# Two channel products by Strassen's scheme, in two sweeps over the batches

## The chip, the cores and the metric

The kernel runs on one core of one Trainium2 chip. A time is device microseconds of that core, from the start of the program to its end. Five engines run beside each other, each through its own instructions in the order written: TensorE (PE; its weight loads are listed as PEld), VectorE (DVE), ScalarE (ACT), GpSimd (POOL), and SyncE (SP), whose queue issues all the DMAs here. They meet at semaphores only.

## The reference

Three blocks follow one another: chunked attention (8 batches, 8 heads, 576 tokens, 64 channels a head, chunks of 64), a gated block, and a mixer. The change touches the last, of which this is all:

```python
xt = x.transpose(0, 2, 1)
h = np.maximum(xt @ w_tok1, 0.0) @ w_tok2          # 576 -> 256 -> 576 tokens
u = x + h.transpose(0, 2, 1)
h2 = np.maximum(u @ w_ch1, 0.0) @ w_ch2            # 512 -> 1536 -> 512 channels
return (u + h2).astype(np.float32)
```

`x` is (8, 576, 512). The two products of the last-but-one line are called the channel products here, the two of `h` the token products.

## The kernel before, in words

Every float32 operand of a product is split into two float32r parts, hi (a copy by ACT) and lo (the remainder, by a subtraction on DVE or POOL), and a product is made of three: hi x hi, hi x lo, lo x hi (`PASSES`), summed in PSUM.

Phase A makes attention and the gated block of all batches; its order of issue is written out in strings of words (`FIRST`, `STEADY`, `LAST`), each word an operation and its block. It also rounds the mixer's weights to float32 and leaves them in DRAM, and each batch's result, channels by tokens, in DRAM (`x2d`). `LAST` overlaps the last gated block with the start of phase B: words `f` and `g` load and split weights, `bl`, `bn` load and transpose token rows of batch 0, `k`, `m` are its token products, `D` copies an output of the gated block out of PSUM.

Phase B is the mixer. It goes through batches, two halves of 288 tokens (`HALF`), and 12 blocks `f` of 128 of the 1536 channels. `b_ch1` (L798, matmuls L804) is 12 matmuls (4 blocks of 128 channels x 3 passes) of 288 columns; ACT and DVE take the relu and split it (L810, L811). `b_ch2` (L815, L823), two blocks later, is 12 matmuls into four PSUM banks that stay open over all 12 blocks; then DVE adds u and transposes (L829, L836), and SP stores. The token products of the next batch stand in between (`b_load` L710, `b_nat` L721, `b_tok1` L738, `b_tok2` L773, which adds x and splits u, L790 to L792). Both weights stay in SBUF, hi and lo; their pieces are split during batch 0 (`b_split`, L82). The main loop sets the order:

```python
    for i, (b, h, f) in enumerate(seq):
        b_ch1(b, h, f)
...
        if i >= 2:
            b2, h2, f2 = seq[i - 2]
            b_ch2(b2, h2, f2)
```

The order of issue is program order on every engine. A tile of a pool waits, when its slot comes round again, until the slot's last users are done; within a tile, waits go by the part that is read or written.

## Time and profile before

| | |
|---|---|
| three runs | 1305.63, 1309.06, 1310.22 us |
| median | 1309.06 us |
| profiled execution: its span (no other time is given for it) | 1307.3 us |
| instructions | 25669 |
| matmuls | 10571 |
| of them channel products (L804, L823) | 2304 + 2304 |
| granted TensorE clock, mean | 0.987 |

The profile is of one execution. Its page gives each engine's busy time, the span in 40 slices, the chain of work that ended last, and groups of instructions: line, engine, operation, tiles (out<-in), shapes, count, then busy time, mean duration in ns, idle time ahead of the group and what ended it. Matmuls are pipelined: the duration of one is a latency, and what a matmul costs in a stream is the step from one to the next. Rows of the timeline begin with start and length in us. Rows by stretch give the stretch and its length, busy time and instructions of PE, PEld, DVE, ACT and POOL, granted clock, DMA share and GB/s.

### The profile page before, as it was taken

Reading aid. Unit: us, or ns where it says so; the run is one execution under the profiler, and the core shown is the slowest. Engines: PE = TensorE matmul, PEld = TensorE weight load, DVE = VectorE, ACT = ScalarE, POOL = GpSimd, SP = SyncE. Lnnn points to the kernel's source line nnn. Section 1 sums busy time; section 2 is a strip of 40 time slices with the busy share of each in tenths; the row PEclk is TensorE's granted clock in tenths of the full one; section 3 lists DMA queues with packets and bytes.
Section 4 is the critical chain, followed back from the end, with each engine's and each line's share of the span. In section 5 each row is a group of like instructions: output and inputs, shape, how many; then the busy total and the mean of one; then the engine's idle time right before and its main releaser. Section 6 shows DMA issues by size and latency. Waiting matters only on the chain.

```text
span 1307.3 us, 25669 instructions
## 1 busy us (share of the span) xinstructions
PE 1259.0 (96%) x10571; PEld 1195.4 (91%) x10571; DVE 662.8 (51%) x1357; ACT 419.1 (32%) x822; POOL 160.8 (12%) x151
## 2 busy tenths in 40 slices
PE   6789999999989999999999999999999999999998
PEld 4588998888888989999999999999999999999998
DVE  6986868596777655357332442433333324423421
ACT  2653536363544343345121221211211212212111
POOL 2743223333233000000000000000000000000000
PEclk7889999999999999999999999999999999999999
DMA  8947274867677330255303203222132042032100
GB/s 170 177 97 155 53 170 98 194 133 180 150 142 172 65 77 20 65 144 172 75 4 69 45 13 57 45 35 45 35 69 45 2 69 45 10 60 45 20 16 22
DMA packets 391993, 106.53 MB, mean 81 GB/s; under 512 B 361794, under 2 KB 376706, under 8 KB 391876
## 3 DMA queue, kind: packets, MB, share of 16 engines
q1 hardware_dynamic: 391876, 104.89, 37.9%
q8 instruction: 83, 1.36, 0.5%
q14 instruction: 34, 0.28, 0.1%
HBM read 78.48 MB, written 26.35 MB: 80 GB/s over the span
## 4 chain that ended last, share of the span: by engine, by line
PE 74%; DVE 12%; DMA 5%; SPq 3%; issue 2%; ACT 2%; POOL 1%; DVEq 0%; POOLq 0%; ACTq 0%
PE ps_a L823 23%; PE ps_c L804 23%; PE ps_s L589 6%; PE ps_o L615 5%; PE ps_v L477 4%; PE ps_u L785 4%; PE ps_h L746 3%; SPq L292 3%; PE ps_u L566 2%; DVE qkT L320 2%; DMA c_f<-ctmp 1%; DVE v L543 1%; DMA qk_raw<-in_k_dram 1%; DVE ctmp L152 1%; DVE sm L364 1%
## 5 line engine op out<-in xcount | busy, mean ns | idle before, releaser
L804 PE MATMUL ps_c<-u,c 128*128 128x288 f32 x2304 | 337.4, 295 | 0.4 <-ACT u L791 0.4
L823 PE MATMUL ps_a<-h,c 128*128 128x288 f32 x2304 | 337.8, 295 | 0.0
L823 PEld LDWEIGHTS ps_a<-h,c 128*128 128x128 f32 x2304 | 316.9, 188 | 4.1 <-issue 1.7
L804 PEld LDWEIGHTS ps_c<-u,c 128*128 128x128 f32 x2304 | 316.9, 189 | 1.2 <-ACT u L791 0.8
L811 DVE SCALAR_TENSOR_TENSOR h<-ps_c,h 128x288 fp32r<-128x288 f32 x192 | 87.3, 455 | 389.5 <-ACT h L810 389.5
L810 ACT ACTIVATE h<-ps_c 128x288 fp32r<-128x288 f32 x192 | 79.0, 411 | 446.3 <-PE ps_c L804 446.3
L589 PE MATMUL ps_s<-ws,vn 128*128 128x288 f32 x768 | 112.1, 302 | 8.6 <-ACT ut L576 6.0
L615 PE MATMUL ps_o<-g,w_out 128*128 128x288 f32 x768 | 110.4, 302 | 9.0 <-ACT x2o L622 8.3
L589 PEld LDWEIGHTS ps_s<-ws,vn 128*128 128x128 f32 x768 | 106.2, 193 | 11.0 <-ACT ut L576 7.7
L615 PEld LDWEIGHTS ps_o<-g,w_out 128*128 128x128 f32 x768 | 105.5, 193 | 10.9 <-ACT x2o L622 9.1
L566 PE MATMUL ps_u<-xt,w_in 128*128 128x288 f32 x768 | 105.8, 296 | 0.0
L566 PEld LDWEIGHTS ps_u<-xt,w_in 128*128 128x128 f32 x768 | 103.3, 189 | 0.9 <-POOL w_in L188 0.2
L477 PE MATMUL ps_v<-w_in,xt 128*128 128x512 f32 x384 | 94.6, 403 | 3.3 <-ACT xt L421 1.9
L477 PEld LDWEIGHTS ps_v<-w_in,xt 128*128 128x128 f32 x384 | 72.4, 191 | 21.5 <-ACT xt L421 2.2
masks.py:197 POOL MEMSET ident<- 128x128 f32 x2 | 0.4, 207 | 681.9 <-DVE xn L729 681.6
L370 POOL TENSOR_TENSOR e<-e,sm 128x512 f32<-128x512 f32 (+1 forms) x40 | 39.1, 977 | 229.3 <-DVE sm L366 193.9
L785 PE MATMUL ps_u<-w,h 128*128 128x288 f32 x384 | 61.0, 295 | 0.3 <-DVE xh L790 0.3
L785 PEld LDWEIGHTS ps_u<-w,h 128*128 128x128 f32 x384 | 54.1, 188 | 0.5 <-DVE xh L790 0.5
L162 POOL TENSOR_TENSOR craw<-craw 128x512 f32<-128x512 f32 (+3 forms) x41 | 41.6, 1014 | 101.7 <-DVE craw L154 51.2
L163 POOL TENSOR_TENSOR ctmp<-ctmp,craw 128x512 f32<-128x512 f32 (+3 forms) x41 | 50.8, 1240 | 3.2
L791 ACT CAST u<-xh 128x288 fp32r<-128x288 f32 x64 | 27.7, 433 | 68.3 <-DVE xh L790 68.3
L746 PE MATMUL ps_h<-xn,w 128*128 128x512 f32 x192 | 49.1, 392 | 0.0
(110 smaller groups left out, 1294.8 us busy)
## 6 DMA issues: line engine op xcount, KB each, us to landing
craw<-in_moe_w_ch_dram SPq DMA_DIRECT2D x24, 512.0 KB, 4.3
x_raw<-x2d SPq DMA_DIRECT2D x160, 64.0 KB, 2.7
qk_raw<-in_q_dram SPq DMA_DIRECT2D x128, 72.0 KB, 3.4
qk_raw<-in_k_dram SPq DMA_DIRECT2D x128, 72.0 KB, 2.9
...
out_dram<-oT SPq DMA_DIRECT2D x240, 36.0 KB, 1.7
...
```

Source lines behind the costliest of these rows:

```text
L162: nc.gpsimd.tensor_tensor(out=f32(high), in0=f32(low), in1=f32(high), op=ALU.mult)
L163: nc.gpsimd.tensor_tensor(out=t, in0=t, in1=f32(high), op=ALU.add)
L477: nc.tensor.matmul(ps, lhsT=self.xt[kc][:, p, 128 * ti:128 * ti + 128], rhs=w_in_t[r][:, kc, DM:2 * DM], start=kc == 0 and n == 0, stop=kc ...
L566: nc.tensor.matmul(ps[:, h, 0:HALF], lhsT=w_in_t[r][:, kc, 128 * m:128 * m + 128], rhs=self.xt[kc][:, p, HALF * h:HALF * h + HALF], start= ...
L589: nc.tensor.matmul(ps[:, h, 0:HALF], lhsT=lhsT, rhs=rhs[:, HALF * h:HALF * h + HALF], start=n == 0, stop=n == len(ops) - 1)
L615: nc.tensor.matmul(ps[:, h, 0:HALF], lhsT=w_out_t[r][:, kc, 128 * m:128 * m + 128], rhs=self.g[p][:, kc, h], start=kc == 0 and n == 0, sto ...
L746: nc.tensor.matmul(ps[kk], lhsT=PB["w1"][r][:, m, ksl], rhs=xn[:, p], start=m == 0 and n == 0, stop=False)
L785: nc.tensor.matmul(ps, lhsT=h1[:, kk, p, 128 * m:128 * m + 128], rhs=PB["w2"][r][:, kk, HALF * h:HALF * h + HALF], start=n == 0, stop=n == 5)
L804: nc.tensor.matmul(ps, lhsT=PB["c1", f // 4][r][:, kc, 128 * (f % 4):128 * (f % 4) + 128], rhs=u[p][:, kc], start=n == 0, stop=n == 11)
L810: nc.scalar.activation(out=h2[:, 0], in_=ps, func=ACTF.Relu)
L811: nc.vector.scalar_tensor_tensor(out=h2[:, 1], in0=ps, scalar=0.0, in1=f32(h2[:, 0]), op0=ALU.max, op1=ALU.subtract)
L823: nc.tensor.matmul(acc[m], lhsT=PB["c2"][r][:, f, 128 * m:128 * m + 128], rhs=h2[:, p], start=f == 0 and n == 0, stop=f == NF - 1 and n == 2)
```

## The change

Each channel product is cut into blocks of half size in its three dimensions: 256 of 512 channels, two column halves of the weight, two halves of the tokens. Instead of eight block products, seven are made, of sums and differences of blocks (`SETS` says which weight block goes with which), and further sums behind them give the four result blocks. A product's matmuls still have 128x128 weights and 288 columns.

Both products no longer go hand in hand. A first sweep goes over all batches and makes h = u @ w_ch1 in three column groups of 2 x 256 (the relu comes with the copy or later, by block), 21 block products of 12 matmuls a batch (`ch1`, `ch1_out`), and stores h to DRAM (`hd`), as u is (`u2d`). A second sweep goes over all batches again and makes the other product, 7 block products of 36 matmuls a batch (`ch2`, `ch2_out`), from h and u loaded back (`h_load`, `u_load`).

- Sums of weight blocks (`Comb`): the six pieces of w_ch1 (pairs for the three groups) and of w_ch2 are loaded, added, split, and added on, on POOL, with the copies on ACT; the first pair during `LAST` (words `y`, in place of the `f` and `g` of channel weights), the second ahead of the sweep, the third in group 1 of batch 0. Those of w_ch2 take the same tiles when the last batch's groups are done with them; the last pair is summed on DVE, and split by DVE and POOL, between the sweeps.
- Sums of u blocks (`comb_u`): on DVE, in the last group of the batch before; remainders on DVE, two of seven on POOL.
- Sums of h blocks (`comb_h`): three products ahead, each on 1728 columns; remainders on DVE, two of seven on POOL. `less(o, x, y)` is max(x, 0) - y.
- Token products (`tok_steps`): 19 steps a batch, one after each block product of the first sweep.
- Results of the last product go out by DVE transposes for all batches; the path by TensorE for the last one (`b_out_last`) is dropped.
- Buffers: 3 PSUM tiles of two banks for the products; 4 slots `c` shared by weight pieces and results on their way out; 3 slots `hb`.

The diff, cut to its core:

```diff
 V0 R0 R1 V1 V2 R3 R2 r1 r0 F U0 G r2 R4 r3 U1 E0 r4 rs rq N0 N3 i0 N1 U2 Q0 i1 E1 U3 open N2
 i2 N4 i4 f0 Q1 f1 i3 bl0 Q3 E2 Q2 Q4 W0 xl0 f2 E3 M0 f3 f4 H0 g0 W1 J0 bl1 M1 W2 g1 W3 g2 g3
-bn0 H1 M2 H2 J1 J2 M3 g4 H3 A0 f5 A1 J3 g5 bl2 B0 bn1 f6 xl1 g6 B1 k0 bl3 k1 f7 bl4 bn2 D0 bn3
-D1 f8 g7 bn4 k2 f9 f10 O2 D2 k3 k4 O3 g8 m0 m1 D3 m2 left m3
+bn0 y0 H1 M2 H2 J1 J2 M3 g4 H3 A0 y1 A1 J3 bl2 B0 y2 bn1 xl1 B1 k0 y3 bl3 k1 bl4 bn2 D0 y4 bn3
+D1 y5 bn4 k2 y6 O2 D2 k3 k4 O3 y7 m0 m1 D3 m2 left m3
...
+    SETS = ((0, 0), (1, 0), (1, 1), (0, 1), (2, 0), (3, 0), (3, 1))
+    NX = (2, 2, 1, 2)
...
+    class Comb:
+        def __init__(self, kind, g, kk, new):
...
+        def load(self):
+            self.a = [self.new() for _ in range(2)]
+            for t, s in zip(self.a, self.src):
+                nc.sync.dma_start(out=t, in_=s)
+        def sums(self, eng):
+            (a1, a2), self.t = self.a, self.new()
+            eng.tensor_tensor(out=self.t[:, 0], in0=a2[:, 0], in1=a2[:, 1], op=ALU.add)
+            eng.tensor_tensor(out=self.t[:, 1], in0=self.t[:, 0], in1=a1[:, 0], op=ALU.subtract)
+        def x(self, s):
+            return {0: self.a[0], 1: self.t, 2: self.a[0][:, 1:2], 3: self.a[1]}[s]
+        def hi(self, s):
+            nc.scalar.copy(out=self.dst[s][:, 0, :, self.kk], in_=self.x(s))
+        def lo(self, s, eng):
+            eng.tensor_tensor(out=self.dst[s][:, 1, :, self.kk], in0=self.x(s),
+                              in1=f32(self.dst[s][:, 0, :, self.kk]), op=ALU.subtract)
+        def s4(self, eng):
+            a = self.a[0]
+            eng.tensor_tensor(out=a[:, 1], in0=a[:, 1], in1=self.t[:, 1], op=ALU.subtract)
+        def s3(self, eng):
+            a1, a2 = self.a
+            eng.tensor_tensor(out=a2[:, 0], in0=a2[:, 0], in1=a1[:, 0], op=ALU.subtract)
+    def new_c():
+        return new_out()[:, 0:512].rearrange("p (x n) -> p x n", x=2)
+    def new_out():
+        return PB["r1"].tile([128, 2 * HALF], F32, tag="c", bufs=4, name="c")
+    def new_w():
+        return PB["r3"].tile([128, 2, 256], F32, tag="wraw", bufs=6, name="wraw")
+    def comb_steps(c, add, low):
+        return [lambda: c.sums(add), lambda: (c.hi(0), c.hi(1)),
+                lambda: (c.lo(0, low), c.lo(1, low)),
+                lambda: (c.s4(add), c.s3(add)), lambda: (c.hi(2), c.hi(3)),
+                lambda: (c.lo(2, low), c.lo(3, low))]
...
             nc.vector.tensor_tensor(out=x[:, m], in0=ps, in1=x[:, m], op=ALU.add)
-            nc.scalar.copy(out=u[0][:, m], in_=x[:, m])
-            nc.vector.tensor_tensor(
-                out=u[1][:, m], in0=x[:, m], in1=f32(u[0][:, m]), op=ALU.subtract)
...
-    def b_ch1(b, h, f):
-        u = uT[b, h]
...
+    def tok_steps(b, nxt):
+        def nat(m):
+            def call():
+                xns[b, m] = b_nat(b, m)
+                if m == 1:
+                    b_load(b, 4)
+            return call
+        def one(m):
+            def call():
+                b_tok1(b, m, xns.pop((b, m)))
+                if m == 1:
+                    for h in range(2):
+                        b_load_xh(b, h)
+                if m == 4 and nxt:
+                    for i in range(4):
+                        b_load(b + 1, i)
+            return call
+        steps = [nat(0), nat(1), one(0), nat(2), one(1), nat(3), one(2), nat(4), one(3), one(4),
+                 lambda: None]
+        return steps + [lambda h=h, m=m: b_tok2(b, h, (m,)) for h in range(2) for m in range(4)]
...
+    def split_u(c, x, eng):
+        hi, lo = parts(c)
+        nc.scalar.copy(out=hi, in_=x)
+        eng.tensor_tensor(out=lo, in0=x, in1=f32(hi), op=ALU.subtract)
+    def comb_u(b, c):
+        x1, x2 = xh[b, 0], xh[b, 1]
+        b11, b21, b12, b22 = x1[:, 0:2], x1[:, 2:4], x2[:, 0:2], x2[:, 2:4]
+        sub = lambda o, x, y: nc.vector.tensor_tensor(out=o, in0=x, in1=y, op=ALU.subtract)
+        if c == 0:
+            split_u(0, b11, nc.vector)
+            sub(b11, b12, b11)
+        elif c == 1:
+            split_u(1, b11, nc.vector)
+            sub(b11, b22, b11)
+        elif c == 2:
+            split_u(2, b11, nc.vector)
+        elif c == 3:
+            split_u(3, b21, nc.gpsimd)
+        elif c == 4:
+            split_u(4, b22, nc.gpsimd)
+        elif c == 5:
+            sub(b12, b12, b22)
+            split_u(5, b12, nc.vector)
+        else:
+            sub(b21, b21, b11)
+            split_u(6, b21, nc.vector)
...
+    def new_ps():
+        return PB["ps_c"].tile([128, 2, 512], F32, tag="c", name="ps_c")
+    def ps_of(i):
+        if i == 3:
+            return cur["ps", 0]
+        if i == 4:
+            return cur["ps", 1]
+        cur["ps", i] = new_ps()
+        return cur["ps", i]
...
+    def ch1(b, g, i):
+        ps = ps_of(i)
+        s, x = SETS[i]
+        w = PB["W"][g][s]
+        u = parts(i)
+        for q in range(2):
+            mm_group(ps[:, q, 0:HALF],
+                     [(w[:, r, x, kk, 128 * q:128 * q + 128], u[p][:, kk])
+                      for kk in range(2) for p, r in PASSES], i not in (3, 4))
+    def ch1_out(b, g, i):
+        ps = cur["ps", {3: 0, 4: 1}.get(i, i)][:, :, 0:HALF]
+        def store(k, t):
+            nc.sync.dma_start(out=hd[b][k][:, 2 * g:2 * g + 2], in_=half(t))
+        add = lambda eng, o, x, y: eng.tensor_tensor(out=o, in0=x, in1=y, op=ALU.add)
+        if i == 0:
+            cur["s1"] = post("s1")
+            nc.scalar.copy(out=cur["s1"], in_=ps)
+        elif i == 1:
+            cur["s5"] = post("s5")
+            nc.scalar.copy(out=cur["s5"], in_=ps)
+        elif i == 2:
+            cur["u"] = post("u")
+            add(nc.vector, cur["u"], ps, cur["s1"])
+        elif i == 3:
+            t = new_out()
+            nc.scalar.activation(out=half(t), in_=ps, func=ACTF.Relu)
+            store(0, t)
+        elif i == 4:
+            t = new_out()
+            add(nc.vector, half(t), ps, cur["u"])
+            store(1, t)
+        elif i == 5:
+            cur["w"] = post("w")
+            add(nc.vector, cur["w"], ps, cur["u"])
+            t = new_out()
+            add(nc.gpsimd, half(t), cur["w"], cur["s5"])
+            nc.scalar.activation(out=t, in_=t, func=ACTF.Relu)
+            store(3, t)
+        else:
+            t = new_out()
+            add(nc.vector, half(t), ps, cur["w"])
+            store(2, t)
...
+    def h_load(b, k):
+        t = hs[b, k] = PB["r3"].tile([128, 6, HALF], F32, tag="h", bufs=5, name="h")
+        nc.sync.dma_start(out=t, in_=hd[b][k])
+    def u_load(b, h):
+        t = us[b, h] = PB["r1"].tile([128, 4, HALF], F32, tag="xh", bufs=4, name="u")
+        nc.sync.dma_start(out=t, in_=u2d[b][h])
+    def comb_h(b, i):
+        t = hbs[b, i] = PB["l"].tile([128, 2, 6, HALF], F32R, tag="hb", bufs=3, name="hb")
+        hi, lo = t[:, 0], t[:, 1]
+        h11, h12, h21, h22 = [hs[b, k] for k in range(4)]
+        def less(o, x, y):
+            nc.vector.scalar_tensor_tensor(
+                out=o, in0=x, scalar=0.0, in1=y, op0=ALU.max, op1=ALU.subtract)
+        x = {0: h11, 1: h11, 2: h11, 3: h21, 4: h22, 5: h12, 6: h21}[i]
+        if i == 1:
+            less(h11, h12, h11)
+        elif i == 2:
+            nc.vector.tensor_tensor(out=h11, in0=h22, in1=h11, op=ALU.subtract)
+        elif i == 5:
+            less(h12, h12, h22)
+        elif i == 6:
+            less(h21, h21, h11)
+        if i == 3:
+            nc.scalar.activation(out=hi, in_=x, func=ACTF.Relu)
+            less(lo, x, f32(hi))
+            return
+        nc.scalar.copy(out=hi, in_=x)
+        eng = nc.gpsimd if i in (4, 6) else nc.vector
+        eng.tensor_tensor(out=lo, in0=x, in1=f32(hi), op=ALU.subtract)
+    def ch2(b, i, m):
+        if m == 0:
+            ps_of(i)
+        ps = cur["ps", {3: 0, 4: 1}.get(i, i)]
+        s, x = SETS[i]
+        h = hbs[b, i]
+        mm_group(ps[:, m, 0:HALF],
+                 [(PB["W"][j][s][:, r, x, kk, 128 * m:128 * m + 128], h[:, p, 2 * j + kk])
+                  for j in range(3) for kk in range(2) for p, r in PASSES], i not in (3, 4))
...
+    def ch2_out(b, i):
+        ps = cur["ps", {3: 0, 4: 1}.get(i, i)][:, :, 0:HALF]
+        res = lambda d, h: us[b, h][:, 2 * d:2 * d + 2]
+        add = lambda eng, o, x, y: eng.tensor_tensor(out=o, in0=x, in1=y, op=ALU.add)
+        if i == 0:
+            cur["s1"] = post("s1")
+            nc.scalar.copy(out=cur["s1"], in_=ps)
+        elif i == 1:
+            cur["s5"] = post("s5")
+            nc.scalar.copy(out=cur["s5"], in_=ps)
+            add(nc.gpsimd, cur["s5"], cur["s5"], res(1, 1))
+        elif i == 2:
+            cur["u"] = post("u")
+            add(nc.vector, cur["u"], ps, cur["s1"])
+            add(nc.gpsimd, cur["s1"], cur["u"], res(0, 1))
+        elif i == 3:
+            t = new_out()
+            add(nc.vector, half(t), ps, res(0, 0))
+            put(b, 0, t)
+        elif i == 4:
+            t = new_out()
+            add(nc.vector, half(t), ps, cur["s1"])
+            put(b, 1, t)
+        elif i == 5:
+            cur["w"] = post("w")
+            add(nc.vector, cur["w"], ps, cur["u"])
+            t = cur["c22"] = new_out()
+            add(nc.gpsimd, half(t), cur["w"], cur["s5"])
+            add(nc.gpsimd, cur["w"], cur["w"], res(1, 0))
+        else:
+            put(b, 3, cur.pop("c22"))
+            t = new_out()
+            for m in range(2) if b == NB - 1 else (slice(0, 2),):
+                add(nc.vector, half(t)[:, m], ps[:, m], cur["w"][:, m])
+                if b == NB - 1:
+                    put(b, 2, t, (m,))
+            if b < NB - 1:
+                put(b, 2, t)
...
+        a, b = get(0), get(1)
+        steps = [comb_steps(x, low, low) for x in (a, b)]
+        todo = [[a.load], steps[0][:2], steps[0][2:4], [steps[0][4], b.load], [steps[0][5]],
+                steps[1][:2], steps[1][2:5], [steps[1][5]]]
+        for f in todo[n]:
+            f()
...
     for m in range(4):
...
+        b_load(1, m)
+    cs1, st1 = combs("c1", 1, new_c)
+    cs1[0].load()
+    b_tok2(0, 1, (0,))
+    b_tok2(0, 1, (1,))
+    step()
+    b_tok2(0, 1, (2,))
+    b_tok2(0, 1, (3,))
+    for f in st1[0][:3]:
+        f()
+    comb_u(0, 0)
+    step()
+    comb_u(0, 1)
+    step()
+    comb_u(0, 2)
+    step(2)
+    comb_u(0, 3)
+    comb_u(0, 4)
+    for f in st1[0][3:]:
+        f()
+    cs1[1].load()
+    step(2)
+    comb_u(0, 5)
+    comb_u(0, 6)
+    for f in st1[1]:
+        f()
+    cs2, st2 = combs("c1", 2, new_c)
...
+    def combs(kind, g, new):
+        cs = [Comb(kind, g, kk, new) for kk in range(2)]
+        return cs, [comb_steps(c, nc.gpsimd, nc.gpsimd) for c in cs]
...
+    def second(j, at):
+        cs, st = combs("c2", j, new_w)
+        fill.setdefault((last, at - 1), []).extend([cs[0].load, cs[1].load])
+        for n in range(6):
+            fill.setdefault((last, at + n), []).extend([st[0][n], st[1][n]])
...
+    for b in range(NB):
+        for n in range(21):
+            g, i = divmod(n, 7)
+            if b == last and n == 0:
+                second(0, 7)
+                second(1, 14)
+                c3, _ = combs("c2", 2, wide_new)
+                for c in c3:
+                    fill.setdefault((last, 2), []).append(c.load)
+            ch1(b, g, i)
+            ch1_out(b, g, i)
+            step()
+            for f in fill.pop((b, n), ()):
+                f()
+            if g == 2 and b < last:
+                comb_u(b + 1, i)
+            if b == last and n == 16:
+                comb_h(0, 0)
+            if b == last and n == 19:
+                comb_h(0, 1)
...
+    for c, low in zip(c3, (nc.vector, nc.gpsimd)):
+        c.sums(nc.vector)
+        c.hi(0)
+        c.lo(0, low)
+    for c, low in zip(c3, (nc.vector, nc.gpsimd)):
+        c.hi(1)
+        c.lo(1, low)
+    comb_h(0, 2)
+    for c, low in zip(c3, (nc.vector, nc.gpsimd)):
...
+    prepared = 3
+    for n in range(7 * NB):
+        b, i = divmod(n, 7)
+        if i == 0 and b < last:
+            h_load(b + 1, 0)
+            for h in range(2):
+                u_load(b + 1, h)
+        for m in range(2):
+            ch2(b, i, m)
+        ch2_out(b, i)
+        if prepared < 7 * NB:
+            comb_h(*divmod(prepared, 7))
+            prepared += 1
+        if i == 3 and b < last:
+            for k in (1, 3, 2):
+                h_load(b + 1, k)
```

More of the change, by code (lines that the diff above doesn't have):

```diff
@@ L771, in b_load_xh, with b_tok2 @@
         xh[b, h] = t
[L773 removed]
+    def b_tok2(b, h, ms):
         h1 = tok[b]
         x = xh[b, h]
[L776 to L779 removed]
         for m in ms:
@@ new lines, in parts @@
+    def parts(c):
+        t = PB["ub"][c // 3]
+        return [t[:, c % 3, p] for p in range(2)]
+    def split_u(c, x, eng):
[24 more added lines that the diff above has]
+            split_u(6, b21, nc.vector)
@@ new lines, in attention_gmlp_mixer, with mm_group @@
+    cur = {}
+    def new_ps():
[7 more added lines that the diff above has]
+        return cur["ps", i]
+    def mm_group(ps, ops, first):
+        for n, (lhsT, rhs) in enumerate(ops):
+            nc.tensor.matmul(ps, lhsT=lhsT, rhs=rhs, start=first and n == 0,
+                             stop=n == len(ops) - 1, skip_group_check=True)
@@ new lines, in attention_gmlp_mixer @@
+    assert not steps and not fill
+    for c in c3:
+        c.new = new_w
+    for c, low in zip(c3, (nc.vector, nc.gpsimd)):
[7 more added lines that the diff above has]
+    for c, low in zip(c3, (nc.vector, nc.gpsimd)):
+        c.s4(low)
+        c.s3(low)
+        c.hi(2)
+        c.lo(2, low)
+        c.hi(3)
+        c.lo(3, low)
+    for h in range(2):
+        u_load(0, h)
```

234 lines of the change are left out of this document (93 added, 141 removed).

## Prediction

> **What bounds the kernel now.** I read the page first (shares, chain of waits), then busy time by stretch, the timeline where a steady stretch shows the pitch, then the groups kept apart by shape for the other engines.
>
> ```profile
> span 1307.3 us, 25669 instructions
> PE 1259.0 (96%) x10571; PEld 1195.4 (91%) x10571; DVE 662.8 (51%) x1357; ACT 419.1 (32%) x822; POOL 160.8 (12%) x151
> ...
> PE 74%; DVE 12%; DMA 5%; SPq 3%; issue 2%; ACT 2%; POOL 1%; DVEq 0%; POOLq 0%; ACTq 0%
> ...
> masks.py:197 POOL MEMSET ident<- 128x128 f32 x2 | 0.4, 207 | 681.9 <-DVE xn L729 681.6
> ```
> ```profile
> 590.90:1303.20 712.30, 711.58 (x5175) 696.42 (x5175) 256.75 (x545) 147.55 (x327) 0.50 (x2) 1.00 0.23 45
> ```
>
> The chain is mostly PE, and from the first channel product (590.9) to the last, PE is busy 711.6 of 712.3 us at full clock, while DVE has 36%, ACT 21% and POOL nothing: it sleeps for 682 us. So this phase is PE's own work, and a product less is time less, as long as nothing else becomes late.
>
> ```profile
> 1285.87 1.75 PE L804 MATMUL ps_c<-u,c 128*128 128x288 f32 x12
> ...
> 1289.05 1.75 PE L804 MATMUL ps_c<-u,c 128*128 128x288 f32 x12
> ```
> ```profile
> L804 PE MATMUL ps_c<-u,c 128*128 128x288 f32 x2304 | 337.4, 295 | 0.4 <-ACT u L791 0.4
> L823 PE MATMUL ps_a<-h,c 128*128 128x288 f32 x2304 | 337.8, 295 | 0.0
> ```
>
> Between the two timeline rows lie 24 matmuls (12 of L804, 12 of L823): 3.18/24 = 0.1325 us each; the 295 ns are a latency.
>
> **What is removed.** Now 2304 + 2304 matmuls of 288 columns. After: first sweep 8 batches x 3 column groups x 7 products x 12 = 2016, second 8 x 7 x 36 = 2016. 576 fewer: **-76.3 us**. Shapes and strides of operands are as before, so I keep the pitch. A product of sweep one lasts 1.59 us, of sweep two 4.77, a batch of sweep two 7 x 4.77 = 33.4.
>
> **What is added, and its prices.** Block sums of weights (POOL, copies on ACT), of u and of h (DVE, ACT, some POOL), sums behind the products, 28 MB of h written and read.
>
> ```profile
> L599 DVE TENSOR_TENSOR ut<-ps_s,ut 128x576 f32<-128x576 f32 x32 | 24.0, 749 | 11.8 <-PE ps_s L589 11.8
> L792 DVE TENSOR_TENSOR u<-xh,u 128x288 fp32r<-128x288 f32 x64 | 29.4, 460 | 31.9 <-ACT u L791 31.9
> L729 DVE TENSOR_TENSOR xn<-nat,xn 128x512 fp32r<-128x512 f32 x32 | 22.2, 693 | 22.1 <-ACT xn L727 22.1
> L836 DVE STREAM_TRANSPOSE oT<-o 128x288 f32<-128x288 f32 x60 | 28.7, 479 | 2.1
> L791 ACT CAST u<-xh 128x288 fp32r<-128x288 f32 x64 | 27.7, 433 | 68.3 <-DVE xh L790 68.3
> L602 ACT CAST g<-ut 128x576 fp32r<-128x576 f32 x32 | 21.5, 673 | 59.9 <-DVE ut L599 59.9
> L163 POOL TENSOR_TENSOR ctmp<-ctmp,craw 128x256 f32<-128x256 f32 x4 | 3.5, 881 | 0.3
> ```
> ```profile
> L82 POOL TENSOR_TENSOR ws<-ws_nat,ws x4: 1402/1497/1971, 67.6 to 82.7; 128x576 fp32r<-128x576 f32 x4
> L188 POOL TENSOR_TENSOR w_out<-ctmp,w_out x2: 1277/1288/1299, 98.2 to 115.0; 128x512 fp32r<-128x512 f32 x2
> L605 DVE TENSOR_TENSOR g<-ut,g x32: 748/759/1722, 99.5 to 568.9; 128x576 fp32r<-128x576 f32 x32
> ```
>
> 576 columns: DVE 0.75, ACT 0.67, POOL 1.40 (its shortest). No row has the 1728 columns of a block of h, so I extend: DVE 0.76 + 4 x (0.76 - 0.46) = 1.96; ACT 0.67 + 4 x 0.24 = 1.63; POOL from 256 (0.88, perhaps lengthened) and 512 (1.29) at least 1.8 ns a column, so 3.5 to 4.0, taken 3.8. A transposition of 576 is about 0.7.
>
> **The price that does not stand in a mean** is the spread of L605, 748 to 1722 ns:
>
> ```profile
> 226.01 0.75 DVE L599 TENSOR_TENSOR ut<-ps_s,ut 128x576 f32<-128x576 f32 x1
> 226.18 1.04 POOL L162 TENSOR_TENSOR craw<-craw 128x512 f32<-128x512 f32 x1 [1.16 <-DVE craw L154]
> ...
> 227.30 1.30 POOL L163 TENSOR_TENSOR ctmp<-ctmp,craw 128x512 f32<-128x512 f32 x1
> ...
> 227.50 1.72 DVE L605 TENSOR_TENSOR g<-ut,g 128x576 fp32r<-128x576 f32 x1 [0.74 <-ACT g L602]
> ```
>
> L599 (one operand in PSUM) takes its 0.75 us beside a POOL operation. L605 (both in SBUF) starts 0.2 us into one, which ends at 228.60, and itself ends 0.62 later at 229.22: it stood still until POOL was done. The Trainium skill's page "SBUF — State Buffer", section "SBUF: two separate sides", says so as a rule: VectorE with two SBUF inputs and GpSimd hold one port pair by turns, for whole instructions; this trace agrees. Were the port shared by rate instead, the loss below in sweep two would come out smaller.
>
> **Sweep two, batch by batch.** All nine differences and remainders that DVE makes of h per batch have two SBUF operands; POOL now works beside them (two remainders of 3.8, four sums of 1.4). The DVE queue in steady state, from the end of product 2: sum 0.75, difference 1.96, wait for ACT's copy 1.63, remainder 1.96 (6.3); sum, transposition, difference (3.4); then, behind product 4, ACT's two copies 3.3 hide sum and transposition, remainder 1.96 (5.2); again 6.3; behind product 6 two transpositions, sum, difference, copy, remainder (7.7). That is 28.9, and product 2 of the next batch, which needs the last remainder, adds 4.8: 33.7, against PE's 33.4. Nothing is spare, and three turns of the port fall into this loop: POOL's remainder of block 4 ends some 1.8 after DVE wants the port, that of block 6 another 2.2, the sums for product 5 another 1.1: 38.8, less about 1 for queued instructions that start early. I take +4.5 a batch, **+32** with the first and last batch; bounds 0 (POOL always falls into DVE's waits for ACT) and 53 (half of POOL's 13.2 a batch, two remainders of 3.8 and four sums of 1.4, on the path).
>
> **Entry to sweep one.** ACT, DVE, POOL and SP each run in the order written.
>
> ```profile
> 615.24 6.16 SPq L716 DMA_DIRECT2D x_raw<-x2d  x12
> ```
> ```profile
> x_raw<-x2d SPq DMA_DIRECT2D x160, 64.0 KB, 2.7
> ...
> w_raw<-c_f SPq DMA_DIRECT2D x24, 256.0 KB, 3.2
> ```
> ```profile
> 587.25 2.57 PE L785 MATMUL ps_u<-w,h 128*128 128x288 f32 x18
> 590.09 1.05 PE L785 MATMUL ps_u<-w,h 128*128 128x288 f32 x6 [0.27 <-DVE xh L790]
> 590.98 1.30 PE L804 MATMUL ps_c<-u,c 128*128 128x288 f32 x7
> ```
>
> ```profile
> 999.81 1.55 PE L746 MATMUL ps_h<-xn,w 128*128 128x512 f32 x6
> 1001.20 1.75 PE L823 MATMUL ps_a<-h,c 128*128 128x288 f32 x12
> ```
>
> Six token matmuls of 512 columns take 1.39 us (the step between these rows). Today products start 3.7 us after the token product's first matmul. In the last stretch of the phase before, copies of weight blocks now stand in ACT's queue ahead of the copies behind the output product and wait for POOL's sums: +2.5 (0 to 6). Then SP issues 16 token loads at 0.51 (8.2) ahead of the next weight block (issue and landing 3.5); POOL's two sums 1.5, ACT's second copy 0.6; only behind that copy stands the first copy of u. From there DVE makes three blocks of u and two token transposes with their remainders, each with ACT in between (9.6), and a token product (1.4) comes before the first channel product: 24.8 after the last token sum, for which PE has 7.4 of work. **+18** (8 to 22).
>
> Next, ACT's copy of the first product's result is queued behind the copies of two weight pieces: POOL's two remainders of u 2.8, differences 1.5, a load that waits for the slot 3.5, sums 1.5, remainders 2.6, differences 1.5, copies 1 to 2. That is 15 from the copy of block 3, PE has four products and a token product: **+9** (0 to 11). The third pair of pieces, in column group 2 of batch 0, does the same in small, with DVE held for a buffer: **+5** (0 to 9). Blocks of u for the next batch, in the last group of batches 1 to 6, beside token work: **+4** (0 to 15).
>
> **Turn to sweep two.** The output weights' sums run on POOL in the last batch: a piece is four sums at 0.75, remainders 1.3, 1.3, 0.75, 1.3, so 7.6; four pieces 30, the sums of two groups 3, a remainder of the fifth pair 1.3, waits for ACT's copies in between some 2: 36. From product 7 of the last batch PE has 14 x 1.59 = 22 to do, and the first product of sweep two needs parts of all six pieces. **+14** (6 to 22).
>
> **Clock.** In the first 30 us, with gaps on PE, the granted clock was 0.77; where gaps stood in the middle of the kernel, 0.94.
>
> ```profile
> 0.00:30.00 30.00, 18.34 (x172) 13.29 (x176) 19.93 (x40) 8.17 (x13) 8.76 (x13) 0.77 0.87 157
> 300.00:330.00 30.00, 27.08 (x240) 25.40 (x239) 17.16 (x37) 11.07 (x24) 10.37 (x9) 0.94 0.78 196
> ```
>
> By the second row a gap of 3 us costs 0.06 x 30 = 2 us more; four long gaps here, some of them where PE would wait anyway: **+4** (0 to 8). The Trainium skill ("TensorE: Matmul & The Clock Gate", "Part 1: The HAM clock gate") has a gap of over some 3.4 us followed by half clock for as long; five gaps would then cost 8.5 and the sum would be 4.5 higher.
>
> The gaps of the old phase go: 712.30 - 711.58 = 0.7, -0.7.
>
> **Costed at nothing.** The DMA rate: sweep two moves 3.5 (h) + 1.2 (u) + 1.2 (out) MB per batch, about 160 GB/s, where the last row above had 196 at 0.78 busy. SP's issues: 32 of output as in
>
> ```profile
> 688.16 7.90 SPq L839 DMA_DIRECT2D out_dram<-oT  x16
> ```
>
> at 0.49, so 16, and 6 loads, of some 38 us; the loads of h wait on SP for a buffer that DVE frees behind product 3, and stand two products ahead of their use. The sums behind the products, in both sweeps, have two products of cover except one: product 6 takes the buffer that product 4's sum frees, one product (1.59) after it, for a sum of 0.75. Without that cover it would cost 1 a group, 24.
>
> **Sum**: -76.3 + 2.5 + 18 + 9 + 5 + 4 + 14 + 32 + 4 - 0.7 = +11.5. The profiled execution's span is 1307.3, 1.8 below the median run of 1309.06, which I put around it: 1307.3 + 11.5 + 1.8 = **1321**.
>
> **Rivals.** (1) *Sweep two keeps PE's pace*, the one-time waits stay: POOL's work falls into the waits for ACT. Then 32 becomes about 4: 1293. For it: the two queues need the port 17.6 + 13.2 = 31 of 33.4 us, so an order without loss exists. Against: both queues are fixed in order, and the loop has no slack. (2) *Most waits are covered*: low ends of the entry (8 + 0 + 0), of the turn (6), sweep two 4, the rest 5: -76.3 + 23 - 0.7 = -54, 1255. For it: 36% DVE and idle POOL before. Against: the order of the queues, counted above. (3) *Sweep one is bound by DVE* too: comb of u, token work and sums in one stretch of seven products, 21 us on DVE with its waits for PE's 17, in all batches rather than the first two; decided when the token work falls into the last group: 6 batches x 4 more, 1345. (4) *The products do not get cheaper*: a pair of PSUM banks per product, alternating, could lengthen the pitch; from 0.144 (plus 9%) on, 4032 matmuls eat 46 of the 76: 1367. Against: no row with two banks shows it, L566 has 296 ns with two banks as L804 has 295.
>
> ```profile
> L566 PE MATMUL ps_u<-xt,w_in 128*128 128x288 f32 x768 | 105.8, 296 | 0.0
> ```
>
> **Chances.** The forecast's case 0.46, between 1300 and 1340; (1) 0.22; (2) 0.14; (3) 0.14; (4) 0.04. 0.3% (4 us) is about what this measurement can tell from no change. (1) and (2) are faster, less a tail of (1); the low edge of the forecast's case falls within 0.3%: faster 0.34, same 0.11, slower 0.55. The 80% range cuts half of (2) and (4) with a bit of (3): 1262 to 1348.
>
> **What would show it.** Right: 4032 matmuls at 0.1325; in sweep two DVE operations of 1728 columns that take 3 us and more beside POOL, a batch of about 38 us, PE waiting for POOL's remainder before product 6 and DVE's before product 2; a gap of some 18 us ahead of the first channel product with ACT waiting for a weight load, another behind it; a gap of 14 at the turn. Wrong: sweep two at 33.4 a batch, or PE waiting on DMA landings of h, or a longer pitch.

## The result, and the profile after

The changed kernel takes 1355.03 us (median of 4 runs, 1353.07 to 1357.21), the kernel before 1308.16 us (4 runs). The ratio is 1.0357, with a 95% interval of 1.0339 to 1.0375: **3.6% slower**. The forecast was 1321. Its profiled execution took 1354.58 us with a span of 1352.7, 45.4 us more than the span before.

The page of the kernel after: span, busy times, and the two groups of channel products (L934 is now the matmul of both sweeps; behind the second bar stands TensorE's idle time ahead of the group and what ended most of it).

```profile
span 1352.7 us, 25149 instructions
...
PE 1212.9 (90%) x9983; PEld 1139.0 (84%) x9983; DVE 852.6 (63%) x1277; ACT 514.0 (38%) x810; POOL 448.5 (33%) x323
...
L934 PE MATMUL ps_c<-hb,wt 128*128 128x288 f32 x2016 | 285.3, 304 | 37.1 <-POOL hb L1026 20.1
...
L934 PE MATMUL ps_c<-ub,wt 128*128 128x288 f32 x2016 | 290.9, 300 | 20.3 <-ACT c L971 11.9
```

The work fell as announced: 4032 channel matmuls for 4608, at a median step of 0.133 us in both sweeps. TensorE is busy 46 us less than before and yet ends 45 us later: it waits. (Its busy time falls by less than the 76 us of work removed, in part because matmuls take longer at a lowered clock: a row of six token matmuls takes 2.93 us at 0.50 in the entry below, where the prediction shows one of 1.55.) Where it waits, the busy time by stretch shows (channel products alone; columns: length, PE, weight loads, granted clock, share of DMA, GB/s). The stretches are batch 0, batches 1 to 6 and batch 7 of sweep one, then batch 0 and batches 1 to 7 of sweep two.

```profile
621.55:690.74 69.19, 38.95 (x253) 37.18 (x253) 0.87 0.40 115
690.74:970.13 279.39, 213.46 (x1513) 205.81 (x1513) 1.00 0.50 147
970.13:1022.75 52.62, 38.25 (x254) 37.07 (x253) 0.89 0.53 190
1022.75:1077.87 55.12, 40.62 (x254) 39.59 (x254) 0.79 0.42 134
1077.87:1344.99 267.12, 244.53 (x1766) 240.88 (x1764) 0.97 0.51 138
```

A batch without token work is 33.4 us at pace. Batches 7 and 0 around the turn should take 66.8 and take 107.7; the seven after them take 38.2 each.

**Sweep two.** The timeline of one batch (start, length, engine and line; in brackets the idle time before and who ended it), and VectorE's longest kind of wait over batches 1 to 7 (total, times, longest):

```profile
1167.71 3.93 POOL L1026 TENSOR_TENSOR hb<-h,hb 128x1728 fp32r<-128x1728 f32 x1
...
1169.93 3.53 DVE L1008 SCALAR_TENSOR_TENSOR h<-h 128x1728 f32<-128x1728 f32 x1
...
1175.24 1.96 DVE L1026 TENSOR_TENSOR hb<-h,hb 128x1728 fp32r<-128x1728 f32 x1 [1.78 <-ACT hb L1024]
...
1182.35 3.87 POOL L1026 TENSOR_TENSOR hb<-h,hb 128x1728 fp32r<-128x1728 f32 x1 [7.60 <-ACT hb L1024]
1183.84 4.20 DVE L1026 TENSOR_TENSOR hb<-h,hb 128x1728 fp32r<-128x1728 f32 x1 [1.84 <-ACT hb L1024]
1186.28 3.99 PE L934 MATMUL ps_c<-hb,wt 128*128 128x288 f32 x28 [2.43 <-POOL hb L1026]
```
```profile
DVE hb L1026 <- ACT hb L1024: 48.4, 27, 1.8
```

An operation of VectorE that takes 1.96 us alone takes 3.53 and 4.20 beside POOL and ends 1.82 and 1.82 us after POOL does: it stands until POOL is done. Product 6 waits 2.43 us for POOL's remainder. And 27 times VectorE stands up to 1.8 us before a remainder, until ScalarE has copied the block.

**The turn.** Stretches by all engines (length, then PE, weight loads, DVE, ACT, POOL; clock; DMA share; GB/s), SP's queue, POOL's first instruction on a second-sweep weight, and ScalarE and TensorE around it:

```profile
980.00:985.00 5.00, 5.00 (x40) 5.00 (x39) 2.27 (x3) 0.19 (x1) 1.43 (x1) 1.00 1.01 420
985.00:990.00 5.00, 5.00 (x40) 5.00 (x39) 0.76 (x1) 1.77 (x3) 0.00 (x0) 1.00 1.01 333
990.00:995.00 5.00, 3.55 (x27) 3.31 (x25) 1.52 (x2) 0.00 (x0) 0.00 (x0) 1.00 1.05 385
995.00:1000.00 5.00, 0.00 (x0) 0.00 (x0) 0.00 (x0) 2.72 (x5) 3.84 (x5) 0.79 0.07 23
1000.00:1040.00 40.00, 22.95 (x120) 21.92 (x121) 16.05 (x15) 14.99 (x24) 35.56 (x32) 0.71 0.34 117
```
```profile
975.66 2.15 SPq L996 DMA_DIRECT2D h<-hd  x4
977.86 2.42 SPq L731 DMA_DIRECT2D w_late<-c_f  x4
980.49 6.74 SPq L957 DMA_DIRECT2D hd<-c  x4
987.63 3.00 SPq L731 DMA_DIRECT2D wraw<-c_f  x4
1000.23 9.43 SPq L957 DMA_DIRECT2D hd<-c  x4
1009.71 2.19 SPq L731 DMA_DIRECT2D wraw<-c_f  x4
```
```profile
996.00 0.72 POOL L735 TENSOR_TENSOR wraw<-wraw 128x256 f32<-128x256 f32 x1 [11.22 <-DMA wraw<-c_f]
```
```profile
995.22 0.62 ACT L742 CAST wt<-wraw 128x512 fp32r<-128x512 f32 x1 [7.34 <-DMA wraw<-c_f]
...
999.56 0.64 ACT L971 ACTIVATE c<-ps_c 128x576 f32<-128x576 f32 x1
```
```profile
1000.26 8.63 PE L934 MATMUL ps_c<-ub,wt 128*128 128x288 f32 x48 [6.71 <-ACT c L971]
...
1019.71 3.25 PE L934 MATMUL ps_c<-ub,wt 128*128 128x288 f32 x12 [5.23 <-ACT c L971]
```

The four loads of h (3.5 MB), 1 MB of late weights and the stores fill the DMA engines for 15 us. The weights that are needed first are issued behind them and behind four stores; POOL gets them at 996. Then POOL works 35.6 of 40 us while VectorE does 16, and the clock is at 0.71. The loads of the second pair of weights stand in SP's queue behind four more stores, which wait for ScalarE's output, until 1009.7; the first of their buffers had come free only 0.9 us earlier. TensorE is stopped in batch 7 already: ScalarE stands 7.34 us for the late weights, its copy of a result out of PSUM (L971) stands behind its copies of these weights, and TensorE waits 6.71 us for that copy and 5.23 us for a later one.

**The entry.** SP issues 16 loads of x rows ahead of the weight load on which ScalarE then waits 8.2 us, and TensorE's clock falls:

```profile
591.75 10.74 SPq L781 DMA_DIRECT2D x_raw<-x2d  x16
602.60 0.95 SPq L731 DMA_DIRECT2D c<-c_f  x2
```
```profile
606.23 0.62 ACT L742 CAST wt<-c 128x512 fp32r<-128x512 f32 x1 [8.20 <-DMA c<-c_f]
```
```profile
613.79 2.93 PE L811 MATMUL ps_h<-xn,w 128*128 128x512 f32 x6 [11.62 <-ACT xn L792]
```
```profile
600.00:606.00 6.00, 2.17 (x6) 1.16 (x4) 0.00 (x0) 0.00 (x0) 0.00 (x0) 0.50 0.72 154
606.00:612.00 6.00, 0.00 (x0) 0.00 (x0) 2.15 (x2) 1.81 (x3) 3.88 (x4) 0.50 1.03 281
...
624.00:630.00 6.00, 4.56 (x28) 3.70 (x27) 4.01 (x4) 1.86 (x4) 3.67 (x4) 1.00 0.82 149
```

### The profile page after: what moved, and what is told of

Same layout as the page of the kernel before. It is cut to its first block, busy times and chain, and to the rows that moved or that the text cites. A ratio compares the mean times of both kernels' runs of the same rounds, so it can differ in the third digit from the quotient of the medians.

```text
span 1352.7 us, 25149 instructions
## 1 busy us (share of the span) xinstructions
PE 1212.9 (90%) x9983; PEld 1139.0 (84%) x9983; DVE 852.6 (63%) x1277; ACT 514.0 (38%) x810; POOL 448.5 (33%) x323
## 5 line engine op out<-in xcount | busy, mean ns | idle before, releaser
L934 PE MATMUL ps_c<-hb,wt 128*128 128x288 f32 x2016 | 285.3, 304 | 37.1 <-POOL hb L1026 20.1
L934 PEld LDWEIGHTS ps_c<-hb,wt 128*128 128x128 f32 x2016 | 280.7, 196 | 41.7 <-POOL hb L1026 22.0
L934 PE MATMUL ps_c<-ub,wt 128*128 128x288 f32 x2016 | 290.9, 300 | 20.3 <-ACT c L971 11.9
L934 PEld LDWEIGHTS ps_c<-ub,wt 128*128 128x128 f32 x2016 | 280.2, 192 | 26.4 <-ACT c L971 12.4
L1024 ACT CAST hb<-h 128x1728 fp32r<-128x1728 f32 x48 | 78.0, 1638 | 197.9 <-DVE h L1008 147.3
L1026 DVE TENSOR_TENSOR hb<-h,hb 128x1728 fp32r<-128x1728 f32 x32 | 84.7, 2648 | 69.0 <-ACT hb L1024 69.0
L370 POOL TENSOR_TENSOR e<-e,sm 128x512 f32<-128x512 f32 (+1 forms) x40 | 38.9, 972 | 229.4 <-DVE sm L366 210.7
L959 POOL TENSOR_TENSOR c<-w,s 128x576 f32<-128x576 f32 x24 | 34.7, 1446 | 199.6 <-DVE w L959 199.6
L477 PEld LDWEIGHTS ps_v<-w_in,xt 128*128 128x128 f32 x384 | 73.6, 194 | 21.4 <-ACT xt L421 2.2
L1026 POOL TENSOR_TENSOR hb<-h,hb 128x1728 fp32r<-128x1728 f32 x16 | 62.3, 3894 | 60.8 <-ACT hb L1024 45.6
L811 PEld LDWEIGHTS ps_h<-xn,w 128*128 128x128 f32 x192 | 37.1, 204 | 29.7 <-ACT xn L792 15.8
L1008 DVE SCALAR_TENSOR_TENSOR h<-h 128x1728 f32<-128x1728 f32 x24 | 61.2, 2551 | 0.0
```

The costliest lines, as they stand in the source:

```text
L477: nc.tensor.matmul(ps, lhsT=self.xt[kc][:, p, 128 * ti:128 * ti + 128], rhs=w_in_t[r][:, kc, DM:2 * DM], start=kc == 0 and n == 0, stop=kc ...
L811: nc.tensor.matmul(ps[kk], lhsT=PB["w1"][r][:, m, ksl], rhs=xn[:, p], start=m == 0 and n == 0, stop=False)
L934: nc.tensor.matmul(ps, lhsT=lhsT, rhs=rhs, start=first and n == 0, stop=n == len(ops) - 1, skip_group_check=True)
L1008: nc.vector.scalar_tensor_tensor(out=o, in0=x, scalar=0.0, in1=y, op0=ALU.max, op1=ALU.subtract)
L1024: nc.scalar.copy(out=hi, in_=x)
L1026: eng.tensor_tensor(out=lo, in0=x, in1=f32(hi), op=ALU.subtract)
```

## The experiments

Each starts from the kernel after. The first eight were run once each, beside a single run of the kernel before (1310.68 us for the first four, 1308.18 for the next four). The part ahead of the channel products, which no edit touches, ended anywhere from 587.2 to 593.0 us, so I read stages rather than totals. They come from the starts of the matmuls: the *entry* from the first matmul of batch 0's second token product to batch 7 of sweep one, the *turn* from there to batch 1 of sweep two, and the mean of the *last seven* batches (33.4 at pace). Where no edit touches a stage, it still varies from run to run: the entry from 381.4 to 383.8, the turn from 107.5 to 108.1, the last seven from 38.2 to 38.8.

| kernel | entry and seven batches | turn (two batches) | last seven, each | time |
|---|---|---|---|---|
| after | 382.6 | 107.7 | 38.2 | 1355.0 |
| no POOL in sweep two | 383.8 | 102.0 | 35.9 | 1338.8 |
| POOL's remainders unread | 381.4 | 101.7 | 38.7 | 1358.4 |
| weights ahead of h | 382.5 | 95.1 | 38.6 | 1347.1 |
| weight ahead of x | 375.8 | 108.1 | 38.5 | 1353.2 |
| order | 382.9 | 104.2 | 34.6 | 1331.0 |
| order, VectorE's remainders | 382.6 | 102.4 | 33.5 | 1318.8 |
| entry | 370.4 | 107.5 | 38.5 | 1347.0 |
| turn | 383.0 | 88.8 | 38.8 | 1339.8 |
| all | 361.5 | 81.2 | 34.0 | 1279.9 |
| all, with two moves | 356.3 | 80.2 | 33.5 | 1271.0 |

**No POOL in sweep two.** The remainders of blocks 4 and 6 and POOL's four sums of results are left out, the high parts are multiplied twice, so the output is not the reference's.

```diff
-        eng = nc.gpsimd if i in (4, 6) else nc.vector
-        eng.tensor_tensor(out=lo, ...)
+        if i in (4, 6):
+            return
+        nc.vector.tensor_tensor(out=lo, ...)
...
-            add(nc.gpsimd, cur["s5"], cur["s5"], res(1, 1))
```

> Sweep two without POOL: the remainders of blocks 4 and 6 are left out (their high part is multiplied twice) and the residual rows that POOL adds are left out, so the output is not the reference's. Theory (POOL sets sweep two's pace, by slowing DVE and by its own late results): a batch of sweep two falls from 38.4 to 33.4-34.5 us, VectorE's 1,728-column operations all stay under 2.1 us, the total falls by 28-38 us to about 1317-1327. Rival (VectorE's queue with its waits for the copies is too long by itself, 28.9 us of work and 4.8 of waiting a batch): a batch stays at 36.5 us or more, the total falls by less than 15 us.

Sweep two by all engines, after and here (columns as in the turn), and VectorE's wait for h here:

```profile
1077.86:1344.95 267.09, 244.50 (x1766) 240.89 (x1764) 191.80 (x125) 82.59 (x61) 123.97 (x42) 0.97 0.51 139
```
```profile
1078.66:1329.65 250.99, 240.52 (x1766) 237.85 (x1764) 163.18 (x126) 84.07 (x62) 0.00 (x0) 0.99 0.56 151
```
```profile
DVE h L1008 <- DMA h<-hd: 10.5, 7, 2.1
```

Without POOL the same operations of VectorE take 163.2 us in place of 191.8, 4.1 a batch less, and none of its 1,728-column operations is over 1.96. So POOL lengthens them, as forecast. But a batch still takes 35.9: between the theories. Of that, 1.5 us is VectorE's wait for h in the last row, which it does not have in the kernel after. If h came in time, a batch would take 34.4 at the least. So POOL's share of the 4.8 us that a batch loses against 33.4 lies between 2.3 and 3.8, and this run does not tell more. VectorE's waits for ScalarE's copies are what they were with POOL:

```profile
DVE hb L1027 <- ACT hb L1024: 48.4, 27, 1.8
```

**POOL's remainders unread.** POOL works as before; products 4 and 6 take the high part in place of its result, so the output is not the reference's.

```diff
-    h[:, p, 2 * j + kk]
+    h[:, 0 if i in (4, 6) else p, 2 * j + kk]
```

> POOL works as in the kernel after, but no product reads its remainders of blocks 4 and 6 (the high part is multiplied twice instead, so the output is not the reference's). Theory A (products wait for POOL's result, 3.9 us behind the copy): a batch of sweep two falls to 33.4-34.5 us as in the run without POOL. Theory B (VectorE is slowed beside POOL, and its queue becomes the bound): operations of 3-5 us remain on VectorE and a batch stays at 36-38.5 us. Both at work: between, 34.5-36 us.

TensorE's waits over the last seven batches, the longest kind, first in the kernel after, then here:

```profile
PE ps_c L934 <- POOL hb L1026: 16.7, 7, 2.4
```
```profile
PE ps_c L934 <- DVE hb L1026: 20.6, 15, 2.1
```

A batch takes 38.7: theory B (0.2 over its range). TensorE now waits for VectorE's remainders instead of POOL's, and no less. The row that names POOL as the releaser showed where the loop surfaced, not what set its length.

**Order.** The difference that the next block needs is formed right behind the remainder before it; so the later h loads can go one product earlier.

```diff
     def comb_h(b, i):
+        split_h(b, i)
+        diff_h(*divmod(7 * b + i + 1, 7))
...
-        if i == 3 and b < last:
+        if i == 2 and b < last:
             for k in (1, 3, 2):
                 h_load(b + 1, k)
```

> Each difference of hidden rows is formed one block earlier, right behind the remainder before it, and the three later h loads of the next batch one product earlier. Theory (VectorE stands idle 1.8 us in each of blocks 1, 2, 5 and 6 while ScalarE copies what it has just formed; the run without POOL still took 35.4 us a batch for that reason): a batch of sweep two falls from 38.4 to 35.5-37 us, the total to 1331-1346. Rival (the exclusion between POOL and VectorE alone holds the pace): a batch stays at 38 us or more, the total within 4 us of 1355.

```profile
1077.34:1319.68 242.34, 238.15 (x1766) 234.77 (x1764) 217.06 (x125) 83.28 (x62) 143.05 (x44) 1.00 0.55 152
```
```profile
DVE hb L1040 <- ACT hb L1038: 17.4, 19, 1.1
```

34.6 a batch, below the theory's range, with POOL's work unchanged. VectorE now stands for ScalarE's copies 17.4 us in place of 48.4 (L1040 and L1038 are the lines that were L1026 and L1024). It meets POOL more often, its operations add up to 217 us in place of 192, and it is still the faster kernel: the lengthened operations cost little once the queue has room for them (the next run, with fewer of them, is 1.1 us a batch faster). What the earlier h loads gave by themselves is not shown.

**Order, and VectorE's remainders.**

```diff
-        eng = nc.gpsimd if i in (4, 6) else nc.vector
+        eng = nc.vector
```

> As the run with the differences one block earlier, and the remainders of blocks 4 and 6 on VectorE, so that POOL keeps only four sums of 576 columns a batch. Theory (both causes add up: POOL's 3.9 us remainders stop VectorE, which has the time for them if it does not wait for copies): a batch of sweep two at 33.5-35.5 us, the total 1316-1333. Rival (VectorE, with 3.9 us more of its own a batch, becomes the bound): a batch at 37 us or more, no better than the run with the order alone.

```profile
1073.62:1308.40 234.78, 234.78 (x1766) 234.51 (x1764) 202.35 (x139) 84.49 (x62) 55.52 (x30) 1.00 0.57 158
```

33.5 a batch: TensorE is busy in the whole stretch. VectorE has 28.9 of 33.5 us to do.

**Weights ahead of h.** The first four second-sweep loads are issued ahead of the h loads.

```diff
-        fill.setdefault((last, at - 1), []).extend([cs[0].load, cs[1].load])
+        loads = [cs[0].load, cs[1].load]
+        if j == 0:
+            fill[last, 0][0:0] = loads
```

> The loads of the first two second-sweep weight pieces are issued ahead of the h loads, not behind them and two stores. Theory (the burst of 3.5 MB h and the queue of SP made these weights late): ScalarE's 7.3 us and POOL's 11.2 us of waiting for them fall under 2 us, POOL's chain starts 8-13 us earlier, and the turn costs 20-26 us in place of 34, the total 1341-1347. Rival (POOL's own chain of sums and remainders, 16 us for the first two pieces and 21 for the next, paces the turn, or the h blocks are late in place of the weights): the total falls by less than 4 us.

```profile
987.14 0.74 POOL L735 TENSOR_TENSOR wraw<-wraw 128x256 f32<-128x256 f32 x1
...
998.66 0.65 ACT L971 ACTIVATE c<-ps_c 128x576 f32<-128x576 f32 x1 [6.29 <-DMA hd<-c]
```

POOL starts 14.6 us into batch 7 in place of 25.9 and waits for nothing; the turn falls by 12.6, 9.1 of it up to the end of the first product of sweep two, as the theory had it (the total is at the edge of its range). The burst is still there, and now delays the stores: ScalarE waits 6.3 us for an output buffer.

**Turn.** All weights loaded early in batch 7 into buffers of their own (those of two h blocks serve the second pair), h loads one by one, sums ahead, remainders shared by VectorE and POOL, column group 2 made within the batch.

```diff
+        at_last(0, *l0)
+        at_last(2, *l1)
+        at_last(4, *l2)
+        at_last(5, *s0[0])
...
+        at_last(7, *h_loads(0, (0,)))
+        at_last(9, *h_loads(0, (1,)))
```

> The turn: all second-sweep weights are loaded early in batch 7, each pair in its own buffers, the h loads spread over the batch, the sums formed ahead, the remainders split between VectorE and POOL, and column group 2 made inside the batch. Theory (the turn's 34 us are the burst of loads, POOL's chain and the buffers that the second pair waits for, and the slow clock behind these gaps): batch 7 and the entry to sweep two cost 8-16 us over products at pace, the total 1329-1337. Rival (the copies of the h blocks and the output copies that stand behind the weights on ScalarE set the turn): it still costs 22 us or more, the total above 1341.

The turn falls by 18.9. Batch 7 and the first product of sweep two cost 13.9 over pace, in the theory's range, where they had cost 34.3. The total, 1339.8, lies between theory and rival: the last batches here happened to take 0.6 more each.

**Weight ahead of x.**

```diff
+    cs1, st1 = combs("c1", 1, new_c)
+    cs1[0].load()
     for m in range(4):
         b_load(1, m)
-    cs1, st1 = combs("c1", 1, new_c)
-    cs1[0].load()
```

> The load of the first piece of column group 1 is issued ahead of the sixteen loads of x, not behind them. Theory (ScalarE stood behind that load for 8.2 us, and the first channel product behind ScalarE): the wait falls under 1 us, the first channel product starts at 611-614 us in place of 621.5, and the total falls by 6-11 us. Rival (the token chain or the products after the first take the time up again, since ScalarE's copies for column group 1 still wait for POOL's sums): the first product moves, product 4 of the batch does not, and the total falls by less than 3 us.

```profile
602.42 0.62 ACT L792 CAST xn<-nat 128x512 fp32r<-128x512 f32 x1 [11.15 <-DVE nat L790]
```

By the total undecided: it fell by 1.9 us, the rival's figure, but the single run lost 2.9 before the entry and 2.6 in sweep two. By stage the theory holds: the entry is 6.8 shorter, and product 4 of the batch, which by the rival does not move, starts 47.7 us after the token product's first matmul, where it was 55.7. ScalarE's wait for the weight is gone; the one for the x rows, which stand behind it, takes its place at 11.2 us.

**Entry.** The weight ahead of x as before, the u blocks ahead of the token steps, the second piece and column group 2 inside batch 0, the latter two products earlier.

```diff
+    comb_u(0, 0)
+    st1[0][0]()
+    for c in (1, 2):
+        comb_u(0, c)
+    for f in st1[0][1:3]:
+        f()
```

> The entry to sweep one: the first weight piece of column group 1 is loaded ahead of the x rows, the u blocks of batch 0 are formed ahead of the token steps and of the copies of weights, the second piece and column group 2 move into the first batch, two products earlier than before. Theory (ScalarE's queue, in which copies that wait for weights and tokens stand ahead of the u blocks, makes the entry late): the first channel product starts at 600-606 us in place of 621.5, product 14 of batch 0 waits under 4 us in place of 8.5, and sweep two starts 15-28 us earlier, the total 1327-1340. Rival (the token chain of batch 1, with its x loads, paces batch 0 wherever the products stand): sweep two starts less than 6 us earlier.

```profile
DVE c L959 <- DMA hd<-c: 6.6, 1, 6.6
DVE c L959 <- POOL c L750: 6.5, 1, 6.5
```

Between the two: the first product starts at 596.9, but the entry with its batches gains 12.3, and sweep two starts 8.7 earlier. Weight pieces and outputs share four buffers, and within the batch each waits for the other.

**All.** Order, VectorE's remainders and turn (the weights of its first two pairs loaded and summed in batch 6 already); at the entry the u blocks first, the second piece in the idle token-activation buffer, column group 2 in idle x buffers, the x rows of batch 2 later. In batches 0 and 7 VectorE makes the result sum that is POOL's elsewhere.

```diff
+    h1_raw = f32(PB["r2"].tile([128, 2, 2, DM], F32R, tag="h1", bufs=1, name="w_h1"))
...
+    for c in (0, 3, 1, 4, 2):
+        comb_u(0, c)
```

> All corrections together: the order and VectorE's remainders of sweep two; the weights of the turn loaded and summed in batches 6 and 7 with the h loads spread; and an entry in which the u blocks of batch 0 go ahead, both pieces of column group 1 are loaded at once into the idle buffer of the token activations, those of column group 2 into idle x buffers, and the x rows of batch 2 later. Theory (the change's own saving of 76 us stands, and entry, batch 0, turn and sweep two had cost some 120 us that are no part of Strassen's scheme): sweep two at 33.4-33.6 us a batch (36-40 us saved), the turn at 4-15 us (19-30 saved), the entry with batch 0 at 10-35 us less than after, the total 1262-1292, faster than before. Rival (the corrections take the same idle time from each other: with a shorter entry or turn the queues wait for loads instead): 1300 or more, no faster than before.

1279.85 us against 1310.38, ratio 0.9767 (0.9744 to 0.9790). The gains add up: against after, 21.1 at the entry, 26.5 at the turn, 28.9 in the last seven batches, together 76.5, where the spans differ by 74.9. The last seven miss what was expected (34.0 each for 33.4 to 33.6): the first of them takes 37.1, the others 33.5. A wait is left at the entry:

```profile
614.40 0.40 ACT L742 CAST wt<-c 128x256 fp32r<-128x256 f32 x1 [4.21 <-POOL c L750]
```
```profile
618.18 2.93 PE L811 MATMUL ps_h<-xn,w 128*128 128x512 f32 x6 [10.17 <-ACT xn L792]
```

**All, with two moves.** ScalarE's token copy ahead of those weight copies, the last h load one product earlier.

```diff
-    for n in range(1, 6):
+    for n in (1, 2):
         for st in st1:
             st[n]()
+    step()
...
+        at_last(19, *h_loads(0, (2,)))
```

> As the run with all corrections, with two moves: at the entry ScalarE makes the token copy of the second x piece ahead of the second halves of the weights of column group 1 (in the run with all corrections it stood 4.2 us behind a sum of POOL, and TensorE 10.2 us behind that copy), and at the turn the last h load is issued one product earlier. Theory (the order of ScalarE's queue still costs 10 us in batch 0): the third product of batch 0 waits under 6 us in place of 14.8 us, batch 0 takes 62-68 us in place of 73.6, the total 1268-1277. Rival (the weights of column group 1, made later, are then awaited by product 7, or the x loads set the pace): batch 0 stays at 71 us or more, the total within 3 us of 1279.9.

```profile
592.95:949.22 356.27, 252.10 (x1764) 242.90 (x1765) 0.98 0.54 157
949.22:1029.41 80.19, 68.94 (x507) 67.30 (x505) 1.00 0.56 190
1029.41:1263.95 234.54, 234.54 (x1766) 234.47 (x1764) 1.00 0.57 158
```

1270.99 us (1269.39 to 1274.49) against 1309.70: ratio 0.9700 (0.9684 to 0.9716). The third product of batch 0 takes 4.7 us in place of 14.8, but the first takes 11.0 in place of 2.9: much of the wait moved there. Batch 0 takes 68.4 in place of 73.6, 0.4 over the expected range. So the change does pay, **3.0%**, when the work around the products is arranged for it.

## Why the prediction was wrong

The sign was right, the size was not: +46 for +11.5. By its own terms, against the spans:

| term | forecast | measured |
|---|---|---|
| 576 matmuls fewer | -76.3 | -76.3 |
| last stretch of the phase before | +2.5 | +0.2 |
| entry, first product | +18 | +23 |
| batch 0 (9 + 5) | +14 | +20.5 |
| u blocks, batches 1 to 6 | +4 | +2.3 |
| turn | +14 | +40.9 |
| sweep two | +32 | +33.3 |
| clock | +4 | in the rows above |
| end of the kernel | 0 | +2.8 |
| old gaps | -0.7 | -0.7 |

The measured column adds up to 46.0 for 45.4. Batches 1 to 6 are 279.4 less 5 x 48.7 and 33.6, what the steady ones take. The entry is the first product's delay of 30.4 us less 7.4 of token work done ahead of it, the turn is 107.7 - 66.8, sweep two 267.1 - 7 x 33.4. The +0.2 is this execution's: in the runs above the same part ended up to 5.5 us later.

**The step that failed is the turn**, +14 for 40.9. The prediction set POOL's chain, 36 us from product 7 on, against 22 us of products that run on beside it, and took 22 as its upper bound. The chain itself was sized about right: its first four pieces took 38.9 us, from 996.0 to 1034.9. Its start and the overlap were wrong. The prediction wrote "Costed at nothing. The DMA rate", and judged that rate by the mean of a batch of sweep two, 160 GB/s. But the loads of h and weights come together, 333 to 420 GB/s for 15 us, and SP's queue puts the weights last: POOL started at 996, not at product 7 (984). And the products did not run on: ScalarE's copies of results stood behind its copies of the late weights, and TensorE waited 11.9 us for two of them in batch 7, which took 19.2 us over pace; batch 0 of sweep two took 21.7 over. The run with the weights ahead of h took 12.6 us back, the one with buffers of their own, split remainders and spread loads 18.9, and the last kernel 27.5. Some of the 27.5 is sweep two's loop in batch 0: with order and VectorE's remainders alone the turn fell by 5.3. How much of the 40.9 each part holds by itself is not shown beyond that.

**Sweep two had the right sum; its split stays open.** Forecast: the loop of VectorE alone 33.7, POOL's turns at the port 4.5, so about 38. Measured: 38.2, and 35.9 without POOL. But 1.5 of the 35.9 is VectorE's wait a batch for the landing of h (10.5 over seven), whose loads the prediction had placed "two products ahead of their use". The kernel after has no such wait, so the loop alone lies between 34.4 and 35.9, and POOL's share between 2.3 and 3.8. More important is what I took as given: the waits for ScalarE's copies, 1.63 us in three places and two copies in a fourth, counted into the 28.9 as if fixed. They are largely a matter of order. Against rival 1, the pace of 33.4, I wrote "both queues are fixed in order"; with the difference one block ahead and the h loads one product earlier (not taken apart), the run measured 34.6, and with VectorE's remainders 33.5.

**The entry and batch 0** were right in kind: ScalarE waiting for a weight load with the first copy of u behind it, then copies of weights ahead of ScalarE's other work. Together 43.5 for 32. One term was summed wrongly: 15 us less four products (6.4) and a token product (1.4) is 7.2, where the prediction took 9. One part of the miss is issue: the 16 loads were taken at 0.51 us each and took 10.74 / 16 = 0.67. Another is **the clock**, forecast at +4 over four gaps, by a row in which it had fallen to 0.94 only. Here a row of six token matmuls, 1.55 us long at full clock, took 2.93 at a clock of 0.50, in the middle of the entry. The Trainium skill ("TensorE: Matmul & The Clock Gate", "Part 1: The HAM clock gate") has half clock after an idle window of some 3.4 us, and full clock after a busy one; the stretches from 600 to 612, with the gap of 11.6 us in them, at 0.50 and the one from 624 to 630 at 1.00 agree with it. How much of each term is clock can't be told from these runs.

The **end** was left out: 7.7 us pass behind the last channel product (1345.0 to 1352.7) where it was 4.9. SP stores the last outputs in many small pieces, and the last sum waits for one of them:

```profile
1345.21 0.46 DVE L1057 TENSOR_TENSOR c<-ps_c,w 128x288 f32<-128x288 f32 x1 [2.75 <-DMA out_dram<-c]
```

Rivals 2 and 4 are out for this kernel (a step of 0.133, no covered waits); rival 3 too: batches 3 to 5 run at 48.7, products and token work at pace. Rival 1's pace is what sweep two reaches with the order and VectorE's remainders.
